# Routing steps of a mixture-of-experts kernel placed by other planned durations, with pauses at PSUM reads and larger sort groups

## The chip, the cores and the metric

The kernel runs on one core of one Trainium2 chip. The metric is device time in microseconds (us); lower is better. The core has a TensorE (PE in the profile, with its weight loads as PEld), a VectorE (DVE), a ScalarE (ACT), a GpSimd (POOL) and a SyncE (SP), each with its own queue of instructions that it works off in order. An instruction that has to wait for another engine holds up everything behind it in its own queue.

## The reference

A causal convolution of seven taps per head makes 28672 tokens of 192 numbers; then every token goes to exactly one of eight experts, each with room for 3584, in the order of the logits, and the expert's two-layer network is applied. Cut to that:

```python
x_unf = x_pad[:, idx, :].reshape(B, S, K, H, group)
x = np.einsum('hk,bskhg->bshg', softmax(weight), x_unf).reshape(B * S, D)
order = np.argsort(-(x @ w_gate).flatten())
for i in order:
    tok, e = i // E, i % E
    if assigned[tok] >= 0 or counts[e] >= cap:
        continue
    assigned[tok] = e
    counts[e] += 1
for e in range(E):
    m = assigned == e
    out[m] = np.maximum(x[m] @ w1[e], 0) @ w2[e]
```

## The kernel before

**Stages.** First the convolution: 16 blocks of 8 matmuls each (tile `cv`), copied out by ACT and stored as `attn`; behind it run transposes on DVE (`aT`), the gate's logits (`pl`, `pt`) and each token's best logit (`M`). Then the experts' network: 56 tiles of 512 tokens, numbered 0 to 55 here. Tiles 0 to 7 are the experts' first tiles and load and split their weights (`raw` to `w` and `dl`, an exact split in two parts) on the way; tiles 8 to 31 and 32 to 55 follow with kept weights.

**A step.** Each tile has eight steps f = 0 to 7, and I write 7.5 for step 5 of tile 7. A step on PE is five matmuls of layer 1 of this tile (`ph`, function `l1`) and four pairs of layer 2 of the tile before (`y`, function `l2`). ACT and DVE take the result of layer 1 apart into `hh` and `hl`, through three PSUM banks `ph`. At steps 2 and 5 of the first tiles PE also transposes the next tile's tokens (`px`), and DVE takes them over (`xa`, `xd`).

**Routing.** Which token goes to which expert is worked out beside all this, by the class `Route`: a threshold from counts (`thresh`, whose counts are the tile `m_x`), counts per expert (`count`, `counts`), places in the lists (`place`, `slots`), a sort by one-hot matmuls (`sort` once, `sort4` three times: DVE makes comparison tiles `oa` in a pool of five buffers, PE multiplies them into a bank, ACT copies it to `X`, SP stores it as `otab` and reads it back turned), `gather` and `tokens`, which end in index lists (`ia`/`ja` for tiles 8 to 31, `ib`/`jb` from tile 32 on). Seven rounds (`rounds`) in between fit a price per expert; their counts are `r_c`, `r_cc`, `r_c8`. PSUM for all of routing is two banks, `bg`.

**What sets the order.** No scheduler: instructions stand in each queue in the order in which the Python program issues them. Routing steps are generators. `Meter` adds up a planned time for PE, DVE and ACT as instructions are issued (lines 31 to 57), and `Steps.hook`, called three to four times in each step, lets the generator go on as long as DVE's planned time is at most 1.8 us past PE's. Where a generator says `yield PEW`, it goes on only when PE's planned time has passed DVE's planned end by 0.8 us (0.3 us in the convolution). So the planned durations decide at which place of PE's queue a routing matmul stands. The plan never reads the clock; if DVE is later than planned, PE waits at the matmul.

At step 30.0 the program reads `jb` for tile 32, and the program issues all that is left of routing there (`bg.drain()`); likewise at tile 6 for `ja`.

Of the kernel before, what the change touches and what calls it, by code (L numbers as in the profile page):

```python
# [7 lines left out]
BF = mybir.dt.bfloat16  # L8
I32 = mybir.dt.int32
FR = mybir.dt.float32r  # L10
AF = mybir.ActivationFunctionType
# [7 lines left out]
PEW, PEA = "pe", "pe after act"  # L19


def size(ap):
    n = 1
    for d in ap.shape[1:]:
        n *= d
    return n


class Meter:
# [5 lines left out]
    def __getattr__(self, op):  # L35
        f = getattr(self.eng, op)
        if op == "dma_start":
            return f

        def call(*a, **k):  # L40
            p = self.pace
            aps = [t for t in (*a, *k.values()) if hasattr(t, "shape") and hasattr(t, "dtype")]
            n = max(map(size, aps), default=0)
            bf = all(t.dtype == BF for t in aps if size(t) > 1)
            if self.name == "pe":
                n = size(aps[2])

                d = n / 2400 * (0.25 if bf and size(aps[1]) == 32 else 1 if aps[2].dtype in (BF, FR) or size(aps[1]) == 32 else 2 if op == "transpose" else 4)
                p.pe += max(d + 0.0025, 0.027 if bf else 0.107)
            elif self.name == "dve":  # L50
                w = 1 if not bf or "reduce" in op else 4 if op in ("tensor_scalar", "tensor_copy") else 2
                p.dve = max(p.dve, p.pe) + max(0.08 + n / 960 / w, 0.18)
            else:
                p.act = max(p.act, p.pe) + 0.12 + n / 1400 + (0.2 if "accum_out" in k else 0)
            return f(*a, **k)  # L55

        return call
# [201 lines left out]
class Route:  # L259
# [167 lines left out]
    def columns(self, h, nt, base):  # L427

        nc, wk = self.nc, self.wk
        V, PE = nc.vector, nc.tensor  # L430
        ps = self.bg()
        PE.matmul(ps[:, 0:8], self.U, self.tot[h], start=True, stop=base is None)
        if base is not None:
            PE.matmul(ps[:, 0:8], self.ones, self.tot[base], start=False, stop=True)
        bi = wk.tile([128, 2, 8], I32, name="c_bi")
        V.tensor_scalar(bi[:, 0], ps[:, 0:8], 128.0, None, op0=OP.add)
        V.tensor_copy(bi[:, 1], ps[:, 0:8])
        V.tensor_scalar(bi, bi, 8, None, op0=OP.arith_shift_right)
        c = wk.tile([128, 2, 8], F32, name="c_f")
        V.tensor_scalar(c[:, 0], bi[:, 0], 2.0, None, op0=OP.mult)  # L440
        V.tensor_scalar(c[:, 1], bi[:, 1], 2.0, 1.0, op0=OP.mult, op1=OP.add)
        oh = self.oh = wk.tile([128, 2, 8, 2, 16], BF, name="c_oh")
        V.tensor_tensor(oh[:, :, :, 0, 0:nt].rearrange("p w e t -> p (w e) t"),
                        self.iq[:, None, 0:nt].to_broadcast([128, 16, nt]),
                        c.rearrange("p w e -> p (w e)")[:, :, None].to_broadcast([128, 16, nt]), op=OP.is_equal)
        V.tensor_scalar(oh[:, :, :, 1, 0:nt].rearrange("p w e t -> p (w e) t"),
                        oh[:, :, :, 0, 0:nt].rearrange("p w e t -> p (w e) t"), self.g1[:, h:h + 1], None, op0=OP.mult)
# [25 lines left out]
    def sort(self, h, nt, base, per=8):  # L473

        nc, wk = self.nc, self.wk
        V, A, PE = nc.vector, nc.scalar, nc.tensor
        O = self.O = wk.tile([128, 128, 16], BF, name="X1")
        q = []
        g0 = z = 0
        free = [0.0, 0.0]  # L480
        while z < 128:

            t = max(q[0][1] + nc.las, free[0] if z % 32 == 0 else 0.0) if q else 0.0
            if q and t <= nc.pe:
                if z == 64:
                    self.columns(h, nt, base)
                a = q.pop(0)[0]
                if z % 32 == 0:
                    ps = self.bg()
                for u in range(per):  # L490
                    c = 16 * (z % 32 + u)
                    PE.matmul(ps[:, c:c + 16], a[:, :, u], self.b[:, :, :, z + u], start=True, stop=True,
                              skip_group_check=True)
                if z % 32 == 32 - per:
                    A.activation(O[:, z - 32 + per:z + per].rearrange("p g w -> p (g w)"), ps, AF.Copy)
                    free = [free[1], nc.act + nc.las]
# [12 lines left out]
            yield  # L509
        yield PEA  # L510

    def sort4(self, h, nt, base):


        nc, wk = self.nc, self.wk
        V, A, PE, S = nc.vector, nc.scalar, nc.tensor, nc.sync
        O = [wk.tile([128, 16, 128], BF, name="X%d" % (v + 1)) for v in range(2)]

        b = self.b.rearrange("p w e (i g) -> p (w e i) g", i=2)
        q = []  # L520
        g0 = z = 0
        free = [0.0, 0.0]
        while z < 8:

            t = max(q[1][1] + nc.las, free[0]) if len(q) > 1 else 0.0
            if len(q) > 1 and t <= nc.pe:
                if z == 4:
                    self.columns(h, nt, base)
                ps = self.bg()
                for v in range(2):  # L530
                    a = q.pop(0)[0]
                    for u in range(2):
                        for c in range(4):
                            j = 2 * v + u
                            PE.matmul(ps[32 * c:32 * c + 32, 128 * j:128 * j + 128],
                                      b[:, :, 32 * (c % 2) + 4 * z + j], a[:, u, :, c],
                                      start=True, stop=True, skip_group_check=True)
                A.activation(O[z // 4][:, 4 * (z % 4):4 * (z % 4) + 4].rearrange("p g q -> p (g q)"), ps, AF.Copy)
                free = [free[1], nc.act + nc.las]
                z += 1  # L540
                if z % 4 == 0:
                    S.dma_start(self.otab[z // 4 - 1], O[z // 4 - 1])
            elif g0 < 128 and len(q) < 5:
                a = self.oh_pool.tile([128, 2, 128, 4], BF, name="oa")
                V.tensor_tensor(a, self.irep4[:, None].to_broadcast([128, 2, 128, 4]),
# [107 lines left out]
    def counts(self, n0):  # L653
# [20 lines left out]
        V.tensor_reduce(self.set[:, 1:2], ps[:, 0:8], axis=AX.X, op=OP.add)  # L674
        V.tensor_copy(self.set[:, 0:1], ps[:, 16:17])
        V.tensor_reduce(b[:, 2:3], ps[:, 24:24 + n0], axis=AX.X, op=OP.min)
        yield

        V.tensor_reduce(b[:, 0:1], self.room, axis=AX.X, op=OP.max)
        V.tensor_tensor(b[:, 1:2], self.set[:, 0:1], self.set[:, 1:2], op=OP.not_equal)  # L680
# [178 lines left out]
    def final(self):  # L859
# [29 lines left out]
        b = wk.tile([128, 11], F32, name="u_b")  # L889
        V.tensor_scalar(b[:, 0:8], ps[:, 0:8], 128.0 * TB, None, op0=OP.not_equal)  # L890
        V.tensor_tensor(b[:, 8:11], ps[:, 8:11], w, op=OP.not_equal)
        yield
        s = wk.tile([128, 1], F32, name="u_s")
        V.tensor_reduce(s, b, axis=AX.X, op=OP.max)
        V.tensor_tensor(self.bad, self.bad, s, op=OP.max)
# [806 lines left out]
```

## Time and profile before

| | us |
|---|---|
| median of 3 runs | 1257.85 (1257.07 to 1260.27) |
| the profiled execution | 1263.32 |
| its span in the trace | 1261.50 |

| engine | busy us | share of the span |
|---|---|---|
| PE | 1211.2 | 96% |
| DVE | 974.1 | 77% |
| ACT | 548.5 | 43% |
| POOL | 534.1 | 42% |

How to read the views: the page cuts the span in 40 slices and gives each engine's busy share in tenths. A windows view gives busy time, granted clock and DMA rate between two points. A waits view sums the idle time of an engine by who ended it. A timeline lists instructions with start and duration; in brackets is the idle time of the engine before, and who ended it. A matmul's duration includes its way through the array, so the next starts before it ends; what a matmul costs PE is the distance between starts. All rows say L55: that is the line in `Meter` through which every instruction is issued, so one goes by tile names.

### The profile page before, as it was taken

The numbers are of one execution on the slowest core, as the hardware profiler recorded it, in microseconds if no ns is written. First come the engines' busy times: TensorE is split into PE (matmuls) and PEld (weight loads), VectorE is DVE, ScalarE is ACT, GpSimd is POOL, SyncE is SP. The second block draws the span as 40 slices with busy tenths as digits, with TensorE's granted clock in tenths as the row PEclk, the third lists the DMA queues.
The fourth block names the chain that finished last, engine by engine and source line by source line (L and its number), as shares of the span: only waits on it lengthen the run. The fifth ranks groups of instructions, "written<-read, shape, count | busy, mean of one in ns | idle before, by whom it ended". The sixth has DMA issues, their size and how long they took to land.

```text
span 1261.5 us, 21753 instructions
## 1 busy us (share of the span) xinstructions
PE 1211.2 (96%) x7702; PEld 1038.5 (82%) x7702; DVE 974.1 (77%) x2131; ACT 548.5 (43%) x1220; POOL 534.1 (42%) x528
## 2 busy tenths in 40 slices
PE   5989998999899999999899999999999999999997
PEld 2445567889799889888788999999999999999997
DVE  7398579899799999989885444777777777777772
ACT  4544655565345435454343333333333333333332
POOL 3000434354455454544534555444444444444422
PEclk9999999999899999999999999999999999999999
DMA  9999898899734443635274645113143232414100
GB/s 240 351 322 311 264 333 281 268 325 283 269 98 132 131 144 118 195 89 185 80 201 131 189 117 171 42 48 130 61 153 105 93 100 98 145 52 150 48 23 28
DMA packets 125188, 205.09 MB, mean 163 GB/s; under 512 B 21440, under 2 KB 85392, under 8 KB 121360
## 3 DMA queue, kind: packets, MB, share of 16 engines
q1 hardware_dynamic: 82464, 127.22, 31.6%
q0 software_dynamic: 21504, 44.07, 11.6%
q10 hardware_dynamic: 21104, 32.34, 7.8%
q8 instruction: 62, 1.02, 0.3%
q14 instruction: 54, 0.44, 0.1%
HBM read 118.64 MB, written 84.93 MB: 161 GB/s over the span
## 4 chain that ended last, share of the span: by engine, by line
PE 75%; DVE 13%; DMA 5%; issue 3%; SPq 1%; POOL 1%; ACT 1%; another core or an unknown queue 0%; DVEq 0%; POOLq 0%; ACTq 0%
PE ph L55 35%; PE y L55 34%; DVE X L55 4%; PE cv L55 3%; DVE hl L55 2%; PE bg L55 2%; DMA raw<-in_moe_w_dram 2%; DMA X<-in_x_dram 1%; DMA wgr<-in_moe_w_gate_dram 1%; DVE aT L55 1%; PE pl L55 1%; DVE oa L55 1%; DVE yo L55 1%; DMA kw<-w 0%; POOL xg L1269 0%
## 5 line engine op out<-in xcount | busy, mean ns | idle before, releaser
L55 PE MATMUL y<-w,hh 128*128 128x384 f32 x1792 | 537.7, 355 | 0.0
L55 ACT ACTIVATE hh<-ph 128x512 fp32r<-128x512 f32 x448 | 268.0, 598 | 478.3 <-PE ph L55 432.3
L55 PE MATMUL y<-w,hl 128*128 128x192 f32 x1792 | 449.6, 251 | 0.0
L55 DVE SCALAR_TENSOR_TENSOR hl<-ph,hh 128x512 fp32r<-128x512 f32 x448 | 307.6, 687 | 156.6 <-ACT hh L55 131.5
L55 PE MATMUL ph<-xa,w 128*128 128x512 f32 x1344 | 396.8, 403 | 0.7 <-DVE hl L55 0.6
L55 PEld LDWEIGHTS y<-w,hl 128*128 128x128 f32 x1792 | 341.9, 191 | 16.6
L55 PEld LDWEIGHTS y<-w,hh 128*128 128x128 f32 x1792 | 337.4, 188 | 22.0 <-issue 3.4
L1344 POOL DMA_INDIRECT out_dram<-yo,ia x128 | 142.5, 1113 | 258.7 <-DVE yo L55 222.4
L55 PEld LDWEIGHTS ph<-xa,w 128*128 128x128 f32 x1344 | 219.1, 189 | 21.8 <-issue 1.5
L1344 POOL DMA_INDIRECT out_dram<-yo,ib x96 | 96.0, 1000 | 220.0 <-DVE yo L55 212.6
L55 PE MATMUL ph<-xd,w 128*128 128x512 f32 x448 | 178.2, 398 | 1.1 <-DVE xd L55 1.1
L55 PE MATMUL ph<-xd,dl 128*128 128x512 f32 x448 | 174.9, 390 | 0.2 <-issue 0.2
L55 DVE STREAM_TRANSPOSE xs<-xg 32x128 f32<-32x128 f32 (+2 forms) x408 | 164.8, 404 | 6.6
L1269 POOL DMA_INDIRECT xg<-attn,ja x128 | 138.8, 1085 | 47.7 <-issue 39.0
L55 ACT ACTIVATE yt<-y 128x192 f32<-128x192 f32 x224 | 73.2, 327 | 103.5 <-PE y L55 84.8
L55 PE MATMUL cv<-X,TH 118*128 118x384 f32 x256 | 100.9, 520 | 16.9 <-DMA X<-in_x_dram 13.7
L1269 POOL DMA_INDIRECT xg<-attn,jb x96 | 103.5, 1078 | 29.3 <-issue 29.3
L55 DVE TENSOR_TENSOR yo<-y,yt 128x192 f32<-128x192 f32 x224 | 79.0, 353 | 41.7 <-ACT yt L55 37.6
L55 PEld LDWEIGHTS ph<-xd,w 128*128 128x128 f32 x448 | 84.4, 188 | 25.2 <-issue 4.7
L55 PEld LDWEIGHTS ph<-xd,dl 128*128 128x128 f32 x448 | 84.6, 189 | 20.2 <-issue 0.5
L55 PEld LDWEIGHTS cv<-X,TH 118*128 118x128 f32 x256 | 45.1, 197 | 50.4 <-issue 14.6
L55 ACT ACTIVATE a<-cv 128x384 f32<-128x384 f32 x128 | 59.8, 492 | 54.5 <-PE cv L55 41.8
(238 smaller groups left out, 886.1 us busy)
## 6 DMA issues: line engine op xcount, KB each, us to landing
attn<-a ACTq DMA_DIRECT2D x16, 1344.0 KB
w<-kw SPq DMA_DIRECT2D x14, 1536.0 KB
w<-kv SPq DMA_DIRECT2D x14, 1536.0 KB
kw<-w SPq DMA_DIRECT2D x48, 256.0 KB
kv<-w SPq DMA_DIRECT2D x32, 384.0 KB
X<-in_x_dram SPq DMA_DIRECT2D x17, 672.0 KB
X<-in_x_dram ACTq DMA_DIRECT2D x15, 672.0 KB
scr<-xs SPq DMA_DIRECT2D x96, 96.0 KB
```

The source lines that it names most:

```text
L55: return f(*a, **k)
L1269: self.nc.gpsimd.indirect_dma_start(out=t[:, b], out_offset=None, in_=self.attn[0:rows], in_offset=bass.IndirectOffsetOnAxis(ap=idx[b], ax ...
L1344: st = self.nc.gpsimd.indirect_dma_start(out=self.out, out_offset=bass.IndirectOffsetOnAxis(ap=idx, axis=0), in_=o, in_offset=None, bounds ...
```

## The change

Three edits. The planned durations of `Meter` are replaced. Three pauses are added: `yield PEW` after the DVE instructions that read a PSUM bank in `columns`, `counts` and `final` (`columns` becomes a generator for that, called with `yield from`). And `sort4` handles two banks at once: it waits for four `oa` tiles, not two, and puts 32 matmuls and two copies into one group, with half as many groups. What is computed is the same.

```diff
-                d = n / 2400 * (0.25 if bf and size(aps[1]) == 32 else 1 if aps[2].dtype in (BF, FR) or size(aps[1]) == 32 else 2 if op == "transpose" else 4)
-                p.pe += max(d + 0.0025, 0.027 if bf else 0.107)
+                d = n / 2400 * (0.25 if bf and size(aps[1]) == 32 else 17 / 16 if aps[2].dtype == FR else
+                                1 if aps[2].dtype == BF or size(aps[1]) == 32 else 2 if op == "transpose" else 4)
+                p.pe += max(d + 0.0025, 0.027 if bf else 0.11)
...
-                p.dve = max(p.dve, p.pe) + max(0.08 + n / 960 / w, 0.18)
+                p.dve = max(p.dve, p.pe) + 0.15 + n / 960 / w
             else:
-                p.act = max(p.act, p.pe) + 0.12 + n / 1400 + (0.2 if "accum_out" in k else 0)
+                p.act = max(p.act, p.pe) + 0.22 + n / 1370 + (0.2 if "accum_out" in k else 0)
...
         V.tensor_copy(bi[:, 1], ps[:, 0:8])
+        yield PEW
         V.tensor_scalar(bi, bi, 8, None, op0=OP.arith_shift_right)
...
-                    self.columns(h, nt, base)
+                    yield from self.columns(h, nt, base)
...
-        free = [0.0, 0.0]
-        while z < 8:
-
-            t = max(q[1][1] + nc.las, free[0]) if len(q) > 1 else 0.0
-            if len(q) > 1 and t <= nc.pe:
...
+        free = 0.0
+        while z < 4:
+
+            t = max(q[3][1] + nc.las, free) if len(q) > 3 else 0.0
+            if len(q) > 3 and t <= nc.pe:
+                if z == 2:
+                    yield from self.columns(h, nt, base)
+                for y in range(2):
+                    ps = self.bg()
...
         V.tensor_reduce(b[:, 2:3], ps[:, 24:24 + n0], axis=AX.X, op=OP.min)
-        yield
+        yield PEW
...
         V.tensor_tensor(b[:, 8:11], ps[:, 8:11], w, op=OP.not_equal)
-        yield
+        yield PEW
```

How that moves instructions is shown at three places of PE's queue. The helper's line is L55 before and L56 with the change.

**First round, the count `r_cc`.** Before, it stands in step 7.5, between the third and the fourth matmul of layer 1:

```order
L55 MATMUL y<-w_3664,hh 128x384
L55 MATMUL y<-w_3664,hl 128x192
L55 MATMUL ph<-xa,w_3790 128x512 x3
L55 LDWEIGHTS ones
L55 MATMUL bg<-r_cc,ones 128x56
L55 MATMUL ph<-xd,w_3790 128x512
L55 MATMUL ph<-xd,dl 128x512
```

Now the same count stands in step 9.2, behind all five matmuls of layer 1:

```order
L56 MATMUL ph<-xa,w_3747 128x512 x3
L56 MATMUL ph<-xd,w_3747 128x512
L56 MATMUL ph<-xd,dl 128x512
L56 LDWEIGHTS ones
L56 MATMUL bg<-r_cc,ones 128x56
L56 MATMUL y<-w_3884,hh 128x384
L56 MATMUL y<-w_3884,hl 128x192
```

It has moved by 13 steps. In DVE's queue the instruction that makes `r_cc` stood between the `hl` of 7.3 and that of 7.4, with two splits of loaded weights (`w<-raw`) close by; now it stands between the `hl` of 9.0 and that of 9.1, where no weights are split any more.

**First `sort4`, the columns.** Before, at the end of step 2.3, the two small matmuls of `columns` (`tot`) stand inside a run of sort matmuls:

```order
L55 LDWEIGHTS X_2244
L55 MATMUL bg<-oa,X_2244 32x128
L55 LDWEIGHTS U
L55 MATMUL bg<-tot_2099,U 128x8
L55 LDWEIGHTS ones
L55 MATMUL bg<-tot_1042,ones 128x8
L55 LDWEIGHTS X_2244
L55 MATMUL bg<-oa,X_2244 32x128
```

Now they stand in step 3.3, with layer 2 ahead and behind, and the next sort matmul comes in the following step:

```order
L56 MATMUL y<-w_2376,hh 128x384
L56 MATMUL y<-w_2376,hl 128x192
L56 LDWEIGHTS U
L56 MATMUL bg<-tot_2146,U 128x8
L56 LDWEIGHTS ones
L56 MATMUL bg<-tot_1042,ones 128x8
L56 MATMUL y<-w_2376,hh 128x384
L56 MATMUL y<-w_2376,hl 128x192
```

Eight layer-2 and five layer-1 matmuls, and the `px` transposes, now lie between `tot` and the next `oa` matmul.

**Convolution, the second count of the threshold.** Before, `m_x` follows the transposed logits `pt` at once:

```order
L55 MATMUL cv<-X,TH 128x384 x2
L55 MATMUL pt<-ident,L 128x128
L55 LDWEIGHTS ones
L55 MATMUL bg<-m_x,ones 128x24
L55 MATMUL cv<-X,TH 128x384 x2
L55 MATMUL pl<-aT,c_mu 32x128 x8
```

Now one convolution matmul stands between them:

```order
L56 MATMUL cv<-X,TH 128x384 x2
L56 MATMUL pt<-ident,L 128x128
L56 MATMUL cv<-X,TH 128x384
L56 LDWEIGHTS ones
L56 MATMUL bg<-m_x,ones 128x24
L56 MATMUL cv<-X,TH 128x384
L56 MATMUL pl<-aT,c_mu 32x128 x8
```

Of the five counts of the threshold, the first keeps its place (after 52 convolution matmuls); the others move from 56, 60, 68 and 73 to 57, 62, 70 and 76. Over all, the last matmul of routing moves from step 24.6 to step 29.4, four steps ahead of the point where `jb` is needed. On SP, the two stores of the second `sort4` now stand around the 1.5 MB load `w<-kv`, where before they stood ahead of it.

More of the change, by code (lines that the diff above doesn't have):

```diff
@@ L521, in sort4 @@
         g0 = z = 0
-        free = [0.0, 0.0]
-        while z < 8:
-            t = max(q[1][1] + nc.las, free[0]) if len(q) > 1 else 0.0
-            if len(q) > 1 and t <= nc.pe:
[L527 to L539, printed above, removed]
+        free = 0.0
[6 more added lines that the diff above has]
+                    ps = self.bg()
+                    for v in range(2):
+                        a = q.pop(0)[0]
+                        for u in range(2):
+                            for c in range(4):
+                                j = 2 * v + u
+                                PE.matmul(ps[32 * c:32 * c + 32, 128 * j:128 * j + 128],
+                                          b[:, :, 32 * (c % 2) + 8 * z + 4 * y + j], a[:, u, :, c],
+                                          start=True, stop=True, skip_group_check=True)
+                    k = 8 * (z % 2) + 4 * y
+                    A.activation(O[z // 2][:, k:k + 4].rearrange("p g q -> p (g q)"), ps, AF.Copy)
+                free = nc.act + nc.las
                 z += 1
-                if z % 4 == 0:
-                    S.dma_start(self.otab[z // 4 - 1], O[z // 4 - 1])
+                if z % 2 == 0:
+                    S.dma_start(self.otab[z // 2 - 1], O[z // 2 - 1])
             elif g0 < 128 and len(q) < 5:
```

## The prediction

> **What bounds the kernel now.** I read the page's slices first, then busy time by windows, then PE's waits, then the places themselves.
>
> ```profile
> PE   5989998999899999999899999999999999999997
> DVE  7398579899799999989885444777777777777772
> ```
>
> PE is at nine tenths nearly everywhere, so it is the bound. DVE stays at nine tenths up to slice 21, as long as routing runs, and only there PE has slices of eight: what can be won lies in them. How much that is, two windows tell: tiles 1 to 24, with routing, and tiles 25 to 54, without.
>
> ```profile
> core 0: us, PE busy (x) PEld busy (x) DVE busy (x) ACT busy (x) POOL busy (x), PEclk, DMA share, GB/s
> 175.88:677.45 501.57, 484.58 (x3134) 429.61 (x3134) 451.42 (x1023) 240.41 (x563) 239.34 (x210) 0.99 0.60 191
> 677.45:1226.25 548.80, 548.80 (x3123) 498.13 (x3121) 388.95 (x813) 210.97 (x421) 249.28 (x240) 1.00 0.31 101
> ```
>
> A tile without routing takes 548.80 / 30 = 18.29 us, a step 2.29. Tiles 1 to 24 would take 439.0 at that pace and took 501.6: 62.5 us more. Of these PE was idle for 501.57 - 484.58 = 17.0. Who ended that idle time:
>
> ```profile
> PE bg L55 <- DVE r_cc L55: 5.5, 4, 3.2
> PE px L55 <- DVE xa L55: 2.1, 2, 1.4
> PE bg L55 <- issue: 2.1, 2, 1.2
> PE bg L55 <- DVE u_b L55: 2.1, 1, 2.1
> PE bg L55 <- DVE c_bi L55: 2.0, 1, 2.0
> PE bg L55 <- DVE k_c L55: 1.2, 1, 1.2
> PE ph L55 <- DVE hl L55: 0.6, 1, 0.6
> PE bg L55 <- DMA X<-otab: 0.6, 1, 0.6
> PE bg L55 <- DVE k_b L55: 0.5, 1, 0.5
> ...
> ```
>
> Nearly all are routing matmuls that PE reached before DVE was done. After the two longest, something else is to be seen, the granted clock (PEclk, the third column from the end), in the stretches that follow them:
>
> ```profile
> 323.00:330.00 7.00, 6.48 (x21) 5.80 (x21) 6.46 (x18) 1.65 (x4) 1.86 (x2) 0.51 0.77 278
> 606.00:610.00 4.00, 3.75 (x14) 2.99 (x14) 3.09 (x8) 0.46 (x1) 0.39 (x1) 0.57 0.29 106
> ```
>
> Behind the wait of 3.2 us (`r_cc`, to 323.5) PE ran at about half clock for 7 us, behind that of 2.1 (`u_b`, to 606.3) for about 3.4. That lost 7 x 0.49 + 4 x 0.43 = 5.1 us. The other 62.5 - 17.0 - 5.1 = 40 us are routing's own matmuls and the `px` transposes, and these the change keeps in full.
>
> **The change, part by part.** *Rounds.* The longest wait has a cause outside routing:
>
> ```profile
> 319.59 0.53 ACT L55 ACTIVATE w<-raw 128x384 fp32r<-128x384 f32 x1 [4.59 <-DMA raw<-in_moe_w_dram]
> 320.15 0.56 DVE L55 TENSOR_TENSOR w<-raw,w 128x384 fp32r<-128x384 f32 x1 [3.18 <-ACT w L55]
> 321.24 1.93 DVE L55 TENSOR_TENSOR X<-X 128x448 bf16<-128x448 bf16 x3
> 323.20 0.26 DVE L55 TENSOR_TENSOR r_cc<-X 128x56 bf16<-128x56 bf16 x1
> ```
>
> Loaded weights came late, DVE stood at their split for 3.2 us, and the count behind it was late by the same. With the change no routing matmul stands in tile 7; the first is in 8.6, after the last split. DVE will still stand there, but what is queued behind it is `hl`, and layer 1 has three `ph` banks, so PE can go on for two steps, 4.6 us, longer than 3.2. The other three `r_cc` waits (2.3) come from DVE lagging its plan; the new plan charges 0.15 us and not 0.08 for each DVE instruction. I take all 5.5.
>
> *Pauses.* `k_c`, `u_b` and `c_bi` (1.2 + 2.1 + 2.0 = 5.3) were each waits of a matmul that reuses a bank right behind the bank's readers. With the pauses one step or more lies between: 1.5 steps at `counts`, one at `final`, one and the `px` transposes at `columns`, so 2.3 us and more against waits of 1.2 to 2.1. I take 5.3. A pause is no instruction, it costs nothing by itself; what it delays is routing, which has room until step 30.0.
>
> *Takeover of tokens.* The two `xa` waits (2.1) came from list and round instructions that stood ahead of `xa` on DVE, one of them long:
>
> ```profile
> 238.39 0.95 DVE L55 RECIPROCAL m_f<-m_f 128x128 f32<-128x128 f32 x1
> 239.66 0.68 DVE L55 TENSOR_TENSOR xa<-px,xa 128x512 fp32r<-128x512 f32 x1
> ```
>
> In the new order `xa` stands directly behind an `hl` in tiles 3, 4 and 5, ahead of these. 2.1.
>
> *Sort groups.* PE executes the same number of matmuls; 32 of them cost about 1.1 us between starts either way:
>
> ```profile
> 647.76 1.18 PE L55 MATMUL bg<-oa,X 128*32 128x128 bf16 x32
> 648.87 0.50 PE L55 MATMUL ph<-xd,w 128*128 128x512 f32 x1
> ```
>
> What can go is the wait `issue`, 2.1, which is at these groups, since a group now starts with all four tiles planned as done; I take 1.5, because two copies by ACT still have to free the banks. Of `hl`, `otab` and `k_b` (1.7) I take half, 0.9. Sum of the idle time: 5.5 + 5.3 + 2.1 + 1.5 + 0.9 = 15.3 of 17.0. With the two long waits their half-clock stretches go too: 5.1.
>
> [...] The rows above show half clock right behind both, and I go by them.
>
> *Convolution.* From 45 to 159 us PE is idle for 7.0, most of it for the five counts, while DVE is nearly full:
>
> ```profile
> 45.00:159.00 114.00, 107.01 (x996) 60.72 (x996) 83.93 (x180) 60.02 (x151) 16.94 (x20) 1.00 0.97 305
> 85.00:95.00 10.00, 8.73 (x70) 4.53 (x70) 9.66 (x25) 4.42 (x11) 0.25 (x1) 1.00 1.07 315
> PE bg L55 <- DVE m_x L55: 4.1, 5, 1.0
> PE pl L55 <- DVE aT L55: 1.4, 1, 1.4
> 69.63 0.97 DVE L55 STREAM_TRANSPOSE aT<-a 128x768 f32<-128x768 f32 x1
> 43.51 1.56 PE cv L55 x4
> ```
>
> Two convolution matmuls (four records) are 1.56 us, one 0.75 or so. The counts move back by up to two of them each, but between some of them DVE now has one transpose more to do, 0.9 us. Count by count the wait goes from 0.8, 0.9, 0.6, 1.0, 0.8 to about 0.8, 0.2, 0.7, 0, 0.6: 1.8 less. With 0.2 for the rest: 2.0.
>
> *What is added.* On SP, the load `w<-kv` now stands between the two `otab` stores of the second `sort4`. What such a neighbour does, the third one shows, which has it already:
>
> ```profile
> 631.82 2.50 SPq L542 DMA_DIRECT2D otab<-X  x2
> 644.07 0.26 PE L55 MATMUL bg<-iq,ones 128*128 128x192 bf16 x1
> 662.54 0.32 SPq L542 DMA_DIRECT2D otab<-X  x1
> 674.13 0.55 PE L55 MATMUL bg<-c_oh,X 128*128 128x24 bf16 x16 [0.56 <-DMA X<-otab]
> ```
>
> With the load ahead, the lists were back 11.6 us after the last store was issued; without it 10 us were enough for no wait. In the new order there are some 8.9 us (3.7 steps and 18 small matmuls, less the copies) from the last copy to `gather`. So between 0, if the load is through by then, and 2.7; the load now starts three steps ahead of that store and not 4 us, so I take 1.0. For weights that come late when PE is ahead, 0.6, bounded below as a rival. POOL gets one 1.3 us split ahead of the first token gathers; these were 5 us early and cover it.
>
> **Sum.** 15.3 + 5.1 + 2.0 - 1.0 - 0.6 = 20.8 us. The profiled execution took 1263.3 (span 1261.5), so 1242.5 for such a one. The median of the runs, 1257.85, lies 5.5 lower; taken from it, the sum gives **1237.0**.
>
> **Rivals.** *Weights take over.* Tiles 1 to 7 load and store most:
>
> ```profile
> 175.88:332.71 156.83, 147.42 (x962) 129.55 (x963) 141.64 (x321) 83.89 (x182) 68.13 (x56) 0.98 0.90 297
> 55.00:65.00 10.00, 10.00 (x88) 5.25 (x87) 6.06 (x12) 5.26 (x15) 0.08 (x1) 1.00 1.06 361
> ACT w L55 <- DMA raw<-in_moe_w_dram: 16.9, 14, 4.6
> ```
>
> If these tiles lose their 9.4 idle and 3.4 half-clock us, the same bytes must move at 297 x 156.8 / 144.0 = 323 GB/s. ACT waits for `raw` already, 16.9 us. Against it: 361 GB/s were reached in the convolution, and tiles 5 and 6 run without PE waiting. If the rate stayed, 12.8 of the 20.8 us would be lost: 1249.8.
>
> *The waits form anew.* DVE is busy 451.4 of 501.6 us in tiles 1 to 24, 90%, and does the same work. If it, not the plan, is behind the waits, PE will wait as long at other places, and only the convolution's 2 us stay: about 1256. Against it: routing may now spread over five tiles more, where DVE had 29% to spare.
>
> *The half clock stays.* If those stretches are not tied to the waits, 5.1 us remain: 1242.1.
>
> *Slower.* A group now takes four of five `oa` buffers, so DVE can make one tile ahead and then, in order, holds `hl` behind it until PE has run the group.
>
> ```profile
> 621.59 2.49 DVE L55 TENSOR_TENSOR oa<-irep,q 128x1024 bf16<-128x1024 bf16 x4
> ```
>
> Four tiles and a group are 2.5 + 1.2 = 3.7 us. While that stays under the 4.6 us that three `ph` banks cover, it costs nothing; where DVE comes to it more than 0.9 us ahead of PE, layer 1 stops. If each of 12 groups cost 3.7 us: 1237 + 44 = 1281. In the new order most `oa` rows stand behind the step in which the group frees them, which speaks against it.
>
> **How the numbers follow.** Forecast 0.70, weights 0.12, waits anew 0.09, half clock stays 0.04, slower 0.05. About 0.3% is what a measurement of this kernel can tell from no change. So faster 0.70 + 0.12 + 0.04 = 0.86, same 0.09, slower 0.05. The range runs from all idle time won (17.0 + 5.1 + 7.0 in the convolution = 29.1: 1228.8) to the case of the weights, 1249.8.
>
> **What would show it.** In the new profile no `r_cc`, `u_b`, `k_c` wait of over 0.5 us and no half clock between tiles 1 and 30; 18.29 us a tile from tile 30 on; steps 9.2 and 3.3 of 2.3 to 2.5 us. I am wrong if PE waits for `hl` around sort groups, if `ACT w <- DMA raw` turns up as PE idle in tiles 1 to 7, or if `gather` in tile 27 waits for `otab` by over 3 us.

## The result, and the profile after

The changed kernel takes 1246.89 us (median of four executions, 1246.71 to 1251.99) against 1258.23 for the one before on the same chip (four executions): a ratio of 0.9918, with a 95% interval of 0.989 to 0.9946. That is 11.3 us less; 20.8 were forecast. The profiled executions differ by 11.3 too (1263.32 and 1251.99; spans 1261.5 and 1250.2).

The page's slices of the changed kernel:

```profile
PE   4999989999999999999999989999999999999997
DVE  7388669889898898989888865777777777777772
```

Of PE's slices of eight in the tiles one is left, slice 24 of 40 (719 to 750 us, with step 29.4 in it); DVE stays at eight tenths and more from slice 7 to slice 23. Busy time by windows of the changed kernel: tiles 1 to 29 (routing now reaches tile 29), tiles 30 to 54, the stretch from the first count of the threshold to tile 1, and a stretch at step 29.4:

```profile
core 0: us, PE busy (x) PEld busy (x) DVE busy (x) ACT busy (x) POOL busy (x), PEclk, DMA share, GB/s
177.13:757.28 580.15, 572.27 (x3655) 509.67 (x3654) 500.34 (x1103) 275.36 (x632) 282.96 (x254) 0.99 0.60 188
757.28:1214.61 457.33, 457.33 (x2603) 415.22 (x2601) 344.60 (x734) 175.52 (x350) 203.15 (x196) 1.00 0.28 93
70.16:177.13 106.97, 101.09 (x949) 60.10 (x949) 86.15 (x181) 56.54 (x142) 23.74 (x26) 1.00 0.95 306
744.65:751.48 6.83, 5.48 (x31) 4.93 (x32) 4.66 (x18) 0.60 (x1) 0.00 (x0) 0.50 0.66 257
```

The same stretches of the kernel before, tiles 1 to 29 and from the first count to tile 1:

```profile
175.88:768.92 593.04, 576.05 (x3654) 512.63 (x3654) 496.04 (x1102) 275.72 (x633) 285.29 (x254) 0.99 0.58 183
67.16:175.88 108.72, 100.70 (x949) 59.49 (x948) 85.35 (x182) 57.34 (x141) 24.55 (x26) 1.00 0.96 302
```

So the difference of the two executions is made up like this: tiles 1 to 29 gain 593.04 - 580.15 = 12.9 us, from the first count to tile 1 1.75 (108.72 - 106.97), the opening ahead of that count loses 3.0 (it comes at 70.16, not at 67.16), and the rest is under 0.4. Up to that count both programs have the same order in every queue, but for one transpose on DVE that stands two places earlier right ahead of it; DVE is 3.0 us late before it comes there. In three repeats of the changed kernel below the count came at 68.4, 67.5 and 69.2. So no instruction that the change moves explains these 3.0 us. They may still not be chance alone: in the four traces with the old durations the count stands at 67.1 to 67.3, in the sixteen with the new ones at 67.0 to 72.6. Why is open.

PE's waits in tiles 1 to 29 of the changed kernel, by who ended them (us in total, times, longest):

```profile
PE bg L56 <- DMA X<-otab: 3.3, 1, 3.3
PE bg L56 <- DMA raw<-in_moe_w_dram: 1.6, 1, 1.6
PE bg L56 <- DVE F L56: 1.3, 1, 1.3
PE bg L56 <- DVE r_cc L56: 0.8, 2, 0.6
PE bg L56 <- issue: 0.3, 1, 0.3
...
```

Of the list of before `xa`, `u_b`, `c_bi` and `k_c` are gone, `r_cc` is down from 5.5 to 0.8 and `issue` from 2.1 to 0.3. Three entries have grown or are new, 6.2 us together: `gather` in step 29.4 waits 3.3 us for the lists read back from `otab`, `gather` in step 4.2 waits 1.6 (the entry `raw`; more on it below), and `settle` (`F`) in step 1.3 waits 1.3. The first has half clock behind it: in the row of 744.65 PEclk is 0.50 for 6.83 us.

Where the 3.3 us come from shows on the queues. This is a timeline of the changed kernel (start, duration, engine, line, operation; SPq is SP issuing DMAs, in order):

```profile
730.67 1.81 SPq L1396 DMA_DIRECT2D scr<-xs  x4
...
735.51 0.45 SPq L1399 DMA_DIRECT2D xs<-scr  x1
736.00 0.59 SPq L546 DMA_DIRECT2D otab<-X  x1
736.70 5.47 SPq L563 DMA_DIRECT2D X<-otab  x8
...
730.97 1.08 ACT L56 ACTIVATE X<-bg 128x512 bf16<-128x512 f32 x2
...
746.00 0.58 PE L56 MATMUL bg<-c_oh,X 128*128 128x24 bf16 x16 [3.32 <-DMA X<-otab]
```

ACT had the last group copied at 732.05 (730.97 + 1.08). The store of it left at 736.00, 3.95 us later: on SP it stood behind the takeover of tile 30's tokens, where the first `xs<-scr` waited for the stores of `scr`: these were issued by 732.48, it left at 735.12, 2.6 us later. Then eight reads; the lists were there 10 us after the store, 13.95 after the copies. PE came to `gather` 10.6 us after them.

The wait in 4.2 is of the same kind, though the view names a load of weights. `gather` multiplies `c_oh` with the lists `X` and reads no weights, and a repeat of the same kernel (`d0_full`, the second row) has nearly the same wait put down to the lists:

```profile
253.71 0.55 PE L56 MATMUL bg<-c_oh,X 128*128 128x32 bf16 x16 [1.64 <-DMA raw<-in_moe_w_dram]
253.74 0.55 PE L56 MATMUL bg<-c_oh,X 128*128 128x32 bf16 x16 [1.80 <-DMA X<-otab]
```

The wait in 1.3 is the weights' (DVE, then PE):

```profile
183.48 0.68 DVE L56 TENSOR_TENSOR dl<-raw,w 64x512 fp32r<-64x512 f32 x1 [3.20 <-ACT w L56]
186.64 0.68 DVE L56 TENSOR_TENSOR F<-LT,m_f 128x512 bf16<-128x512 f32 x1
...
187.38 0.25 PE L56 MATMUL bg<-ones,F 128*128 128x1 bf16 x4 [1.34 <-DVE F L56]
```

DVE stood 3.2 us at a split, and `F` behind it was late, as `r_cc` was in tile 7 before.

### The profile page after: what moved, and what is told of

It is laid out like the page before. It is cut to its first block, busy times and chain, and to the rows that moved or that the text cites. A ratio compares the mean times of both kernels' runs of the same rounds, so it can differ in the third digit from the quotient of the medians.

```text
span 1250.2 us, 21752 instructions
## 1 busy us (share of the span) xinstructions
PE 1208.1 (97%) x7702; PEld 1036.5 (83%) x7702; DVE 979.4 (78%) x2131; ACT 547.4 (44%) x1220; POOL 531.7 (43%) x528
## 4 chain that ended last, share of the span: by engine, by line
PE 85%; DVE 6%; DMA 5%; issue 1%; SPq 1%; ACT 1%; POOL 1%; ACTq 0%; POOLq 0%; DVEq 0%
PE ph L56 40%; PE y L56 38%; PE bg L56 3%; PE cv L56 3%; DMA X<-in_x_dram 2%; DVE X L56 1%; DVE aT L56 1%; DMA wgr<-in_moe_w_gate_dram 1%; DMA raw<-in_moe_w_dram 1%; DMA X<-otab 1%; PE pl L56 1%; DMA xg<-attn,ja 1%; DVE hl L56 0%; PE px L56 0%; DMA otab<-X 0%
## 5 line engine op out<-in xcount | busy, mean ns | idle before, releaser
L56 PE MATMUL y<-w,hh 128*128 128x384 f32 x1792 | 536.8, 355 | 0.0
L56 ACT ACTIVATE hh<-ph 128x512 fp32r<-128x512 f32 x448 | 267.2, 597 | 486.3 <-PE ph L56 485.2
L56 PE MATMUL y<-w,hl 128*128 128x192 f32 x1792 | 449.7, 251 | 0.0
L56 DVE SCALAR_TENSOR_TENSOR hl<-ph,hh 128x512 fp32r<-128x512 f32 x448 | 308.5, 689 | 138.6 <-ACT hh L56 134.0
L56 PE MATMUL ph<-xa,w 128*128 128x512 f32 x1344 | 395.6, 402 | 0.0
L56 PEld LDWEIGHTS y<-w,hl 128*128 128x128 f32 x1792 | 341.7, 191 | 16.4
L56 PEld LDWEIGHTS y<-w,hh 128*128 128x128 f32 x1792 | 337.1, 188 | 20.4 <-issue 2.2
L56 PEld LDWEIGHTS ph<-xa,w 128*128 128x128 f32 x1344 | 218.9, 189 | 20.2 <-issue 1.0
L1348 POOL DMA_INDIRECT out_dram<-yo,ia x128 | 138.9, 1085 | 225.9 <-DVE yo L56 188.1
L56 PE MATMUL ph<-xd,w 128*128 128x512 f32 x448 | 178.9, 399 | 1.3 <-DVE xd L56 1.3
L56 PE MATMUL ph<-xd,dl 128*128 128x512 f32 x448 | 174.6, 390 | 0.2 <-DVE dl L56 0.2
L56 DVE STREAM_TRANSPOSE xs<-xg 32x128 f32<-32x128 f32 (+2 forms) x408 | 164.8, 404 | 6.6
L56 PE MATMUL cv<-X,TH 118*128 118x384 f32 x256 | 101.5, 523 | 19.5 <-DVE TH L56 12.5
L56 ACT ACTIVATE yt<-y 128x192 f32<-128x192 f32 x224 | 73.1, 326 | 94.3 <-PE y L56 92.3
L56 DVE TENSOR_TENSOR yo<-y,yt 128x192 f32<-128x192 f32 x224 | 79.5, 355 | 41.3 <-ACT yt L56 39.2
L56 PEld LDWEIGHTS ph<-xd,w 128*128 128x128 f32 x448 | 84.3, 188 | 21.4 <-DVE xd L56 1.7
L56 PEld LDWEIGHTS ph<-xd,dl 128*128 128x128 f32 x448 | 84.5, 189 | 19.7 <-issue 0.5
L56 PEld LDWEIGHTS cv<-X,TH 118*128 118x128 f32 x256 | 45.3, 198 | 49.9 <-issue 14.1
L56 ACT ACTIVATE a<-cv 128x384 f32<-128x384 f32 x128 | 59.5, 492 | 50.8 <-PE cv L56 33.0
```

Of the source, the lines that this page charges most:

```text
L1348: st = self.nc.gpsimd.indirect_dma_start(out=self.out, out_offset=bass.IndirectOffsetOnAxis(ap=idx, axis=0), in_=o, in_offset=None, bounds ...
```

## The experiments

Each was timed in five rounds beside the kernel before, several kernels side by side on one chip. The chips differ (the kernel before took 1260 to 1272 us on them), so ratios are compared, and kernels that ran on the same chip first. The kernel before was profiled on the first chip only; a wait that is missing in a trace of another chip is therefore compared across chips.

### Which part brings the time

Each of the three edits alone, and all but one; the diffs are the ones of the change, taken apart.

**Durations alone** (`a1_durations`), against the kernel before; PE's durations change too, as in the change:

```diff
...
-                p.dve = max(p.dve, p.pe) + max(0.08 + n / 960 / w, 0.18)
+                p.dve = max(p.dve, p.pe) + 0.15 + n / 960 / w
...
-                p.act = max(p.act, p.pe) + 0.12 + n / 1400 + (0.2 if "accum_out" in k else 0)
+                p.act = max(p.act, p.pe) + 0.22 + n / 1370 + (0.2 if "accum_out" in k else 0)
```

> Only the planned durations are new. If the parts add up as in the sum of the prediction (theory SUM), this part brings the rounds (5.5), the xa waits (2.1), the half-clock stretch at tile 7 (3.4) and the convolution (2.0), less 0.6 for weights: 12.4 us, 1245.8 against 1258.2. If each part mainly moves everything behind it and the waits form anew where they then fall (theory MOVED), the k_c, u_b and c_bi waits or others take part of that back: 4 to 8 us, 1250 to 1254.

Measured: 0.9877 (0.985 to 0.9904), 1252.06 against 1267.22: 15.2 us less, more than SUM gave to this part. In its trace the three `r_cc` waits left make 2.3, `k_c` is gone, `u_b` is 0.6, `c_bi` waits 2.8.

**Pauses alone** (`a2_pauses`): the three `yield PEW` and the generator `columns`.

```diff
+        yield PEW
...
-                    self.columns(h, nt, base)
+                    yield from self.columns(h, nt, base)
...
```

> Only the three pauses are new. SUM: the waits k_c, u_b and c_bi (5.3) and the half-clock stretch behind u_b (1.7) go, the r_cc waits stay: 7.0 us, 1251.2 against 1258.2. MOVED: those three waits go, but the steps behind them stand elsewhere and new waits of several us appear, or a gather now waits for its otab: within 3 us of before.

Measured: 1.0016 (0.9998 to 1.0034), 1270.24. PE's waits in tiles 1 to 29 of this kernel:

```profile
PE bg L55 <- DVE r_cc L55: 6.5, 4, 2.9
PE bg L55 <- DVE oa L55: 2.5, 3, 1.4
PE bg L55 <- ACT X L55: 2.3, 2, 1.5
...
```

The interval includes 1, that is, no change. `k_c`, `u_b` and `c_bi` are gone as they should, and others are there in their place: MOVED.

**Groups alone** (`a3_groups`): `sort4` of the change, without pause.

```diff
-        while z < 8:
+        while z < 4:
...
-            t = max(q[1][1] + nc.las, free[0]) if len(q) > 1 else 0.0
+            t = max(q[3][1] + nc.las, free) if len(q) > 3 else 0.0
...
```

> Only the larger sort groups are new. SUM: about 2.4 us (the issue waits at the sort groups and part of hl and otab): 1255.8 against 1258.2. MOVED: the last otab store falls behind other work on SP and its gather waits, 3 us or more, with half clock behind it: slower than before by 1 to 5 us.

Measured: 1.0047 (1.0025 to 1.0069), 1273.26: slower. Its waits:

```profile
PE bg L55 <- DVE r_cc L55: 5.2, 4, 1.8
PE bg L55 <- DMA X<-otab: 3.8, 1, 3.8
...
```

The last `gather`, in 25.3 here, waits 3.8 us for `otab`, as MOVED had it (granted clock of this execution 0.995 in the mean). So the groups can bring such a wait by themselves. They are not alone in that: with the durations alone the last `gather`, in 27.4, waits 1.8 and 3.5 in two of three traces. PE also waits for `hl` here, four times, 2.5 in sum, but not between the groups of a sort.

**Pauses and groups, old durations** (`a4_no_durations`):

```diff
...
-                p.dve = max(p.dve, p.pe) + 0.15 + n / 960 / w
+                p.dve = max(p.dve, p.pe) + max(0.08 + n / 960 / w, 0.18)
...
```

> Pauses and larger groups with the old durations. SUM: 7.0 + 2.4 = 9.4 us, 1248.8 against 1258.2, and the r_cc wait of 3.2 us in tile 7 is still there. MOVED: less than the two parts alone together, by 3 us or more, with a new wait named in the trace.

Measured: 0.9953 (0.9934 to 0.9972), 1260.25: 7.0 us less, where the two alone were 3.0 (not clear of noise) and 6.0 more. This is 2.4 short of SUM and far better than the two parts alone; neither theory had it. The `r_cc` wait of 3.2 us that was to stay is not there either: there are five, the longest 1.6, 5.7 in sum. Parts do not add, in either direction.

**Durations and pauses** (`a5_no_groups`), the old `sort4`:

```diff
...
-        while z < 4:
+        while z < 8:
...
```

> New durations and the pauses, old sort groups. SUM: the larger groups are worth 1.5 to 2.4 us, so this is that much slower than the full change (ratio 0.992 where that has 0.990). MOVED, from the earlier runs (groups alone +6 us, pauses alone +3): without the larger groups the last gather stands elsewhere on SP, its wait of 2.5 to 3.3 us changes place or goes, and this is 0 to 4 us faster than the full change (0.987 to 0.990).

**Durations and groups** (`a6_no_pauses`), without the three pauses:

```diff
...
-        yield PEW
...
```

> New durations and larger groups, no pauses. SUM: the k_c, u_b and c_bi waits are back, 5.3 us, with half clock behind the longest, 1.7: 7 us slower than the full change (0.9955). MOVED: the new durations have already put other work between those places, one or two of the three waits stay under 0.7 us and this is within 3 us of the full change (0.988 to 0.992).

**Durations alone, again** (`a1_durations_2`), the edit of `a1_durations`:

> New durations alone once more, on the chip of the other runs of this call. Earlier: 0.9877 (0.985 to 0.9904) on another chip, where the time before was 9 us longer. If pauses and larger groups add nothing to the durations, within 3 us of the full change, 0.988 to 0.992; if they add the 9.4 us of SUM, 0.9975.

Measured side by side on one chip: durations and pauses 0.9908 (0.989 to 0.9926), durations and groups 0.9898 (0.988 to 0.9917), durations alone 0.9861 (0.9835 to 0.9886). Neither pauses nor groups bring anything beside the durations here. Without the groups the ratio lies between what SUM and MOVED gave. Without the pauses MOVED holds: `k_c` and `u_b` do not appear, `c_bi` makes 0.9 in two waits.

**The full change and the durations alone on one chip** (`d0_full`, `d1_durations`, edits as above):

> The full change, beside the next three on one chip. 0.988 to 0.993 of before.

> New durations alone, on the same chip as the full change. NOTHING ON TOP (the pauses and larger groups add nothing or cost): equal to the full change or up to 6 us faster. SUM: 9.4 us slower than it. If the earlier difference came from the chips: within 2 us of it.

Measured: full change 0.9902 (0.9874 to 0.9931), durations alone 0.9897 (0.9868 to 0.9926); 1255.58 and 1254.51 us. The two are equal, so NOTHING ON TOP holds: the durations carry the whole gain. What is left for the pauses then is to be seen in the waits of the durations alone (tiles 1 to 29):

```profile
PE bg L56 <- DVE r_cc L56: 2.6, 4, 1.4
PE bg L56 <- DVE oa L56: 1.4, 1, 1.4
...
PE bg L56 <- DVE u_b L56: 0.6, 1, 0.6
```

`k_c` and `c_bi` are not in its list, and `u_b` is down from 2.1 to 0.6, without any pause. In the other two executions of this kernel `c_bi` waited 2.8 and 0.8 us, so there the pause in `columns` would have something to win.

### The waits that were left

**The full change again** (`b0_again`, no edit):

> The changed kernel once more, beside the next three. Theory PLAN (the waits that are left come from the order itself): the gather in step 29.4 waits for otab by about 3.3 us again, the one in 4.2 by 1 to 2, settle in 1.3 by about 1.3, the token transposes before layer 1 for xg by about 1.6; half clock follows the longest. Theory CHANCE (that execution was unlucky): two or more of the four are under 0.5 us. The time: 0.989 to 0.995 of before as first measured, or less if chance had a part.

Measured: 0.99 (0.9875 to 0.9926), 1248.15. The waits come back in every execution of this kernel that was profiled (four): in 29.4 3.3, 2.5, 3.0 and 3.1 us, in 4.2 1.6, 1.3, 1.8 and 1.6. So PLAN holds for the gathers; the one for `F` lay between nothing and 1.3, the one for the tokens (`xg`) between nothing and 2.4.

**The stores of `otab` on ACT's queue** (`b1_act_store`):

```diff
-                    S.dma_start(self.otab[z // 2 - 1], O[z // 2 - 1])
+                    A.dma_start(self.otab[z // 2 - 1], O[z // 2 - 1])
```

> As the changed kernel, but the otab stores are issued on ACT's queue, not SP's. Theory QUEUE (in 29.4 the second store stood 3.95 us on SP behind reads of xs that wait for the stores of scr): the store is issued at once behind the copies, the gather in 29.4 waits under 0.5 us, no half clock behind it: 5.4 us less than the change. Theory ROUND TRIP (store and turned reads need over 10.6 us in themselves): the wait stays over 2 us and the time within 2 us of the change's. The gather in 4.2 gains 0.8 at most either way.

Measured: 0.9902 (0.9877 to 0.9926), 1247.03; no gain. Its timeline:

```profile
729.29 0.34 ACTq L546 DMA_DIRECT2D otab<-X  x1
...
734.04 4.07 SPq L563 DMA_DIRECT2D X<-otab  x8
...
742.43 0.58 PE L56 MATMUL bg<-c_oh,X 128*128 128x24 bf16 x16 [2.55 <-DMA X<-otab]
```

The store left at once, behind the copies, as QUEUE said. The reads did not: they still stood on SP behind `xs<-scr`, to 734.04, and from the first read to the matmul it was 8.4 us. QUEUE named the right queue, and the wrong instruction in it: the wait stays, at 2.55. ROUND TRIP is right in the wait and the time; of its 10.6 us this run shows the eight reads' 8.4, from the first read to the matmul.

**`gather` planned 14 us behind the copies** (`b2_turn14`):

```diff
-TURN = 10.0
+TURN = 14.0
```

> As the changed kernel, but gather is planned 14 us, not 10, behind the last copy: steps 4.4 and 29.7 for 4.2 and 29.4. Theory PLAN: both waits go (3.3 + 1.6) and the half clock behind the first (2.1): 7.0 us less than the change. Rival NEXT WAIT: jb is then ready too late for tile 32 and PE waits for xg or px around steps 30.6 to 31.5 by 2 us or more: within 3 us of the change.

Measured: 0.9896 (0.987 to 0.9922), 1248.08. In 4.4 there is no wait any more. The last sort starts later now, and its `gather` stands at 29.7, right ahead of the deadline at 30.0; there it waits 2.3 us (SP, then PE):

```profile
738.72 0.58 SPq L1231 DMA_DIRECT2D w<-kw  x1
...
739.89 0.58 SPq L546 DMA_DIRECT2D otab<-X  x1
740.51 12.70 SPq L563 DMA_DIRECT2D X<-otab  x8
...
755.90 0.55 PE L56 MATMUL bg<-c_oh,X 128*128 128x24 bf16 x16 [2.31 <-DMA scr<-xs]
```

The second store now stands behind the 1.5 MB load `w<-kw`, and the reads take 12.7 us to issue. The view names `scr<-xs`, which this matmul does not read either; that it was the lists again is likely, not shown. Neither theory had this wait, and the waits that NEXT WAIT named are not there. In the trace tiles 1 to 29 take 575.4 us, 3.8 less than in `b0_again` (granted clock of both executions 0.995 in the mean), and the first count of the threshold comes 4.3 us later (72.6 for 68.4). So the edit does help in the tiles of this execution; why the median shows nothing is open.

**Half of the reads early** (`c1_early_reads`): the reads of the first `otab` go behind its own store.

```diff
                     S.dma_start(self.otab[z // 2 - 1], O[z // 2 - 1])
+                    if z == 2:
+                        self.OT = wk.tile([128, 16, 128], BF, name="X1")
+                    self.back(z // 2 - 1)
...
```

> As the full change, but sort4 issues its first four turned reads of otab behind the first store, six steps before, and only four behind the second. QUEUE and ROUND TRIP have each a part by now: the reads stand behind the reads of xs on SP, and eight of them take 8.3 us from first issue to landing. With four the lists are back 2.5 to 4 us earlier: the waits in 29.4 (2.5 to 3.3) and 4.2 (1.3 to 1.6) go to under 0.7 each, the half clock behind the first with them: 3.5 to 5.5 us less than the full change, 0.986. If instead what lands last is set by other transfers (w<-kw, raw) at that time, the waits stay over 1.5 us and the time within 1 us of the full change.

Measured: 0.9896 (0.9875 to 0.9918), 1260.51 against 1272.17; no gain in sum, as far as the ratios on other chips tell. In 29.4 the wait is 0.6 as expected. In 4.2 it is 4.1 (granted clock of this execution 0.995 in the mean); SP in tiles 3 and 4:

```profile
230.22 0.32 SPq L546 DMA_DIRECT2D otab<-X  x1
234.61 1.79 SPq L568 DMA_DIRECT2D X<-otab  x4
...
246.71 0.59 SPq L546 DMA_DIRECT2D otab<-X  x1
252.66 1.82 SPq L568 DMA_DIRECT2D X<-otab  x4
```

Each read that waits for its own store holds SP (4.4 and 5.9 us here), and in these tiles SP has the weights to load and store.

**Token gathers ahead of the weight splits on POOL** (`b4_gather_first`):

```diff
-                if i >= 14 and h % 2:
+                if i >= 14 and h % 2 and got:
                     ff.wsplit(-1, P)
```

> As the changed kernel, but POOL splits no weights ahead of the token gathers: the two splits there go behind the eight gathers. Theory PORT (DVE's four index operations took 1.26, 1.21, 0.74 and 0.66 us while those two splits ran on POOL, and about 0.2 each before, with no split beside them): they are back to about 0.2, ja is 3.2 us earlier, the gathers start 2 to 3 us earlier, the waits for xg (1.65) go: 1.6 us less than the change. Rival SPLIT LATE: w or dl of tile 0 is then late and layer 1 waits for it by 1 to 3 us: no gain or a loss of up to 2 us.

Measured: 0.9935 (0.9913 to 0.9957), 1253.07: 4.9 us slower than the full change on that chip. PORT held for the operations and for the gathers, which start 2.5 us earlier; its time did not. SPLIT LATE is not the reason: PE waits only 0.3 for `dl`. In the changed kernel DVE's index operations stood beside POOL's splits:

```profile
141.71 1.26 DVE L56 TENSOR_SCALAR m_i<-m_f,off 128x32 int32<-128x32 f32 x1
143.01 1.21 DVE L56 SCALAR_TENSOR_TENSOR m_y<-m_i,m_y 128x32 f32<-128x32 int32 x1
...
141.65 1.29 POOL L1254 TENSOR_TENSOR w<-raw,w 128x512 fp32r<-128x512 f32 x1 [32.54 <-ACT w L56]
```

Without the splits they are short, but ACT then waited ahead of `xd`:

```profile
141.46 0.23 DVE L56 TENSOR_SCALAR m_i<-m_f,off 128x32 int32<-128x32 f32 x1
141.73 0.19 DVE L56 SCALAR_TENSOR_TENSOR m_y<-m_i,m_y 128x32 f32<-128x32 int32 x1
...
161.59 0.59 ACT L56 ACTIVATE xd<-bg 64x512 fp32r<-64x512 f32 x1 [3.37 <-DMA kd<-dl]
...
162.95 0.80 PE L56 MATMUL ph<-xd,w 128*128 128x512 f32 x1 [4.30 <-DVE xd L56]
```

The copy `xd` does not read `kd`. What stands just ahead of it on ACT is the store of `attn`, issued at 161.19; what that waited for no run shows. Layer 1 began 1.9 us earlier (88.4 us behind the first count, 90.3 in `b0_again`), and tile 0 took 5.4 longer (21.4 for 16.0), with 6.83 us at half clock in it that `b0_again` does not have (granted clock of the two executions 0.989 and 0.995 in the mean).

### Two repairs

**Early reads in the later two sorts, and 14 us for the first** (`d2_both_fixes`, and again as `e1_both_fixes` beside `e0_full`, the full change):

```diff
+                    if nt == TB:
+                        if z == 2:
+                            self.OT = wk.tile([128, 16, 128], BF, name="X1")
+                        self.back(z // 2 - 1)
...
-        self.there = nc.act + TURN
+        self.there = nc.act + (TURN if nt == TB else 14.0)
...
```

> The full change with two repairs: in the second and third sort4 the first four turned reads go behind the first store, and behind the first sort4 gather is planned 14 us after the last copy, not 10. If the missing gain is the two gather waits: the wait in 29.4 is under 0.7 (shown alone before), the gather now in 4.4 waits under 0.5 (shown alone before), and the time is 4 to 5 us less than the full change. If each repair only moves the waits: within 1.5 us of it.

> The full change once more, as the partner of the next run: 0.988 to 0.993 of before; step 29.4 waits 2.5 to 3.3 us again, with half clock behind it.

> The full change with the two repairs once more. If the waits in 29.4 and 4.2 are a part of the missing gain: 2 to 5 us less than the full change, as before (2.7 by the means). If what they free is lost to other waits: within 1 us of it.

Measured: 0.9879 (0.9853 to 0.9905) beside the full change's 0.9902, and 0.9871 (0.9847 to 0.9895) beside 0.9908 (0.988 to 0.9935): 1.5 and 4.6 us less by the medians, where 4 to 5 and 2 to 5 were expected. The intervals of a pair overlap; both pairs point the same way, and so do the traces: tiles 1 to 29 take 3.4 and 4.7 us less than in the full change beside them. PE's waits in tiles 1 to 29 of the second of these (`e1_both_fixes`):

```profile
PE bg L56 <- DMA X<-otab: 1.6, 2, 1.1
...
```

and the windows view of the same stretch:

```profile
174.63:751.04 576.41, 570.79 (x3654) 507.44 (x3654) 497.53 (x1103) 275.66 (x632) 283.74 (x253) 1.00 0.60 189
```

The wait in 29.4 is 1.1 (1.3 in `d2_both_fixes`; under 0.7 was expected), the one in 4.2 is gone, and there is no half clock: PEclk is 1.00. At 1246.00 against 1262.34 before, the ratio is the lowest of those with all three edits. It is not below the durations alone: on the chip of `d2_both_fixes` these took 1254.51 for its 1254.07, and their lowest ratio is 0.9861.

**Early reads on the durations alone** (`d3_durations_early`): the same edit to the old `sort4`.

```diff
                     S.dma_start(self.otab[z // 4 - 1], O[z // 4 - 1])
+                    if nt == TB:
+                        if z == 4:
+                            self.OT = wk.tile([128, 16, 128], BF, name="X1")
+                        self.back(z // 4 - 1)
...
```

> The new durations alone, with the first four turned reads behind the first store in the second and third sort4. The gather in 27.4 waited 1.8 and 3.5 us for otab in the two executions of the durations alone: it waits under 1 us, 2 to 4 us less than the durations alone (with the half clock behind it). If reads on SP then hold up the loads behind them: no gain.

Measured: 0.9923 (0.9897 to 0.9949), 1258.33 against 1254.51 for the durations alone: 3.8 us more by the medians, with intervals that overlap. SP around tile 27:

```profile
697.03 0.45 SPq L1244 DMA_DIRECT2D w<-kv  x1
697.59 0.37 SPq L543 DMA_DIRECT2D otab<-X  x1
706.04 1.79 SPq L570 DMA_DIRECT2D X<-otab  x4
```

The second store stands right behind the load `w<-kv`, and 8.4 us pass until its reads go out: `gather` waits 7.3. Going by the wait, the same edit gains in one order and loses in another, by what stands ahead of it on SP.

## Why the forecast was right in direction and too large

Term by term, in us, for the profiled pair (tiles 1 to 29 unless said):

| term of the prediction | forecast | measured |
|---|---|---|
| rounds, `r_cc` | 5.5 | 4.7 (5.5 to 0.8) |
| pauses: `k_c`, `u_b`, `c_bi` | 5.3 | 5.3 (all gone) |
| `xa` | 2.1 | 2.1 |
| sort groups, `issue` | 1.5 | 1.8 (2.1 to 0.3) |
| `hl`, `otab`, `k_b` 0.9; added at `otab` -1.0; weights -0.6 | -0.7 | -4.5 (1.7 to 6.2) |
| half clock | 5.1 | 2.4 (5.1 to 2.7) |
| convolution | 2.0 | 1.75 |
| opening, not in the sum | 0 | -3.0 |

The measured rows add up to 10.6; 0.8 of the 11.3 has no row.

**The waits that I named went, in this execution.** The places were right: steps 9.2 and 3.3 took 2.4 us each, tile 7 18.29, tiles from 30 on 18.29. The half clock behind `r_cc` and `u_b` went with them (from 34.7 to 1246.4 us the one stretch below full clock is that of 744.65), so the rival that it stays is out. The 4.7 of `r_cc` does not hold on every chip. In traces of the full change and of the variants closest to it the `r_cc` waits made 0.2 to 0.9 on the chips where the kernel before took 1258 to 1262 us. In the three from the slower chips they made 3.5, 3.7 and 2.8 (`d0_full`, `c1_early_reads`, `d2_both_fixes`; granted clock of these executions 0.996, 0.995 and 0.995 in the mean). What differs there is not shown.

**The step that failed is "What is added".** It asked of one `gather`, that of tile 27, whether its lists would be back, found a load between the stores on SP, and took 1.0. That `gather` waited 0.3 (0.8 in `d0_full`): its lists were used 9.9 us after the last store, with that load ahead, where the prediction had 11.6. The one in 4.2 and the last one, in 29.4, I did not ask about. They waited 1.6 and 3.3, and behind the second came half clock, 2.7 more by its row, an estimate ((6.83 - 1.35) x 0.5; 1.35 of the stretch lie in the wait). In place of 1.0 the gathers thus cost 7.9. Repairing these two gave 1.5 and 4.6 us on the chip. The ten us that "were enough for no wait" counted from the store; in 29.4 the store left 3.95 us behind the copies from which the plan counts.

**"Weights" was somewhat small.** 0.6 was taken. The 1.3 in 1.3 is a late split, and PE waits 0.2 for a `dl`; the rest of the -4.5 is the gathers'. The rival that the weights take all of it (12.8) was far off: tiles 5 to 7 have no wait.

**The pauses' 5.3 and the groups' 1.5 are counted in the right place and put down to the wrong cause.** The trace after has them, as forecast; the runs show that the durations alone remove most of the same waits, that pauses alone bring nothing and groups alone cost 6.0, and that on top of the durations the two bring nothing. The sum was made as if each wait belonged to one edit. One explanation that fits is that most of them came from one thing, DVE later than planned: the edit that mends the plan takes them, and moving one place while the plan is wrong lets the wait form at the next. This is argued, not shown. The edit changes the durations of PE, DVE and ACT together, and they were not tried apart. Nor was a plan that is as wrong but places the steps elsewhere. That another order can gain under the old plan, `a4_no_durations` shows with its 7.0. The rival "the waits form anew" was right for pauses and for groups, each alone.

**Convolution.** The counts gained 2.8 (`m_x` 4.1 to 1.3). "These were 5 us early and cover it" was wrong: DVE's index operations beside the two splits took longer (the first two 1.26 and 1.21 us, 0.23 and 0.19 before), the gathers started later (at 146.34, not at 143.78), and PE waited 1.5 for the tokens. In sum 1.75, by luck near the 2.0.

**The rival "slower"** did not come: no `hl` wait stands at the sort groups of the changed kernel.

The 9.5 us that are missing are in the main 3.8 of waits that formed anew, 2.7 of half clock and 3.0 of the opening of that execution, whose cause is open. Without the opening the pair would differ by 14.3; the four timed comparisons of the full change (0.9918, 0.99, 0.9902, 0.9908) give 10 to 13.

## What to carry to other kernels

Gains of several edits on the same waits do not add: run each alone, and count on top of the first only what is left, here nothing. Where the waits seem to have one cause, such as an engine later than its plan, try the edit of the plan first. Whoever moves work to other steps has to follow every round trip through memory that moves with it, not one of them, on the queue that issues it: what stands ahead of the store, ahead of the reads, and what big load lies right before. In this kernel a wait costs its length; where PE was idle for 1.8 us or more of one 3.41 us window, half clock came next in 23 of 23 cases (below), by my estimate up to 1.7 us more for each window of it.

## What the runs showed of the hardware

**Half clock came behind windows in which PE had idled long.** But for the one at the very end of the kernel (5.33 us before, 5.83 with the change), its stretches last 3.41 or 6.83 us in every trace, and they begin on one grid per execution: in the kernel before at 322.98 and 606.29, 283.31 us apart, which is 83.0 times 3.413. Windows of that grid in the kernel before:

```profile
319.57:322.98 3.41, 0.76 (x4) 0.38 (x3) 2.76 (x5) 3.12 (x7) 1.49 (x1) 1.00 0.97 341
322.98:329.81 6.83, 6.29 (x20) 5.61 (x20) 6.32 (x17) 1.67 (x4) 1.67 (x2) 0.50 0.76 271
602.88:606.29 3.41, 1.32 (x14) 1.01 (x14) 1.21 (x7) 0.08 (x1) 2.80 (x3) 1.00 0.67 179
213.76:217.17 3.41, 1.96 (x22) 1.47 (x22) 3.27 (x12) 0.53 (x2) 2.23 (x2) 1.00 0.98 346
```

In the first PE idles 3.41 - 0.76 = 2.65 us, in the third 2.09, and the next windows run at half clock; in the last it idles 1.45, though the wait at its start (`c_bi`, 2.0 us, lying across two windows) is nearly as long as that of `u_b`, and nothing follows. In the changed kernel the window ahead of 744.65 (741.24 to 744.65) has 1.97 us of idle time, and PEclk is 0.50 behind it. Over all twenty traces, of the windows at full clock between 60 and 1230 us: with 1.8 us of idle time or more, half clock came next in 23 of 23; with 0.6 to 1.2, in 0 of 146; between, in 9 of 69. In the profiled pair alone it is 3 of 3, 0 of 16 and 0 of 7. A window at clock 0.50 costs up to 3.41 x 0.5 = 1.7 us, an estimate from these rows.

**Two short DVE operations took as long as POOL's beside them.** 1.26 and 1.21 us in the changed kernel, in the stretch in which POOL ran two splits of 1.29 and 1.27, instead of 0.23 and 0.19 without the splits (`b4_gather_first`). The first of these DVE operations ends at 142.97, POOL's first split at 142.94. What held DVE up is not shown.

**512 KB in turned reads took 8.4 us** from the first read to the matmul that needs them (742.43 - 734.04 in `b1_act_store`), with other loads on the queues and beyond the store itself.
